# FNet mixing and an RWKV channel mix in one kernel: K by whole pieces, two small operations moved between engines, one pair of gathers gated, some value products earlier

## The chip, the cores and the metric

The kernel runs on one NeuronCore of a Trainium2 chip. The metric is the device time of one execution, in microseconds. The core has five engines with a queue of instructions each: TensorE (PE in the profile, with its weight loads as PEld), VectorE (DVE), ScalarE (ACT), GpSimd (POOL) and SyncE (SP, here for output transfers only). Each works through its own queue in order and waits on semaphores for the others. Data moves between memory and the chip by 16 DMA engines; the transfers issued by GpSimd go through one queue (q0), those by SyncE through another (q1). TensorE writes into PSUM; VectorE and ScalarE carry results from there to SBUF ("evict").

## The reference, cut to what matters

```python
def _attn_ref(x):                       # x: (8, 3072, 256)
    X = np.fft.fft(x, axis=1)
    X = np.fft.fft(X, axis=2)
    return X.real.astype(np.float32)

def _moe_ref(x, mu_k, mu_r, w_k, w_v, w_r):
    x_prev = np.concatenate([np.zeros((B, 1, D)), x[:, :-1, :]], axis=1)
    xk = mu_k * x + (1.0 - mu_k) * x_prev
    xr = mu_r * x + (1.0 - mu_r) * x_prev
    k = np.maximum(xk @ w_k, 0.0)       # w_k: (256, 1024)
    v = k * k @ w_v                     # w_v: (1024, 256)
    r = 1.0 / (1.0 + np.exp(-(xr @ w_r)))   # w_r: (256, 256)
    return (r * v).astype(np.float32)
```

The output of the first function is the x of the second. The real part of a two-dimensional Fourier transform is taken for each of 8 batches, neighbouring rows are mixed, and a squared-ReLU layer with a sigmoid gate follows.

## The kernel before

**The transform.** It is done with matrix products and symmetry. The sequence of 3072 is split as 48 x 64. For each batch the rows of x and their mirror images are added (`fold`, into the tile p, VectorE), multiplied by tables of cosines and sines over the 48 (`a_sum`, `a_item`, `a_half`: into the tile a), multiplied by tables over the 256 columns (`d_units`, `d_item`, `d_small`: into g_all), and multiplied by tables over the 64 (`c_sums`, `c_item`, `c_pairs`: into y, which has 27 slots of 2 x 64 columns). `turned` repairs one column of g_all by a permutation. `evac` copies PSUM to SBUF on VectorE ("V") or ScalarE ("A"). Neighbouring slots of y are subtracted (`diff`, into d), scaled by mu (`scaled`, into t) and combined (`mixed`, into the tiles x), which gives xk and xr in transposed form, 128 partitions by 2 halves by 1536 columns; the "halves" are the two halves of the 256 columns of the model.

**The tables** are made on the chip at the start: angles are formed from small matrix products in PSUM, scaled and offset to a whole number of turns, wrapped by a bit-and, and put through the sine. `m_angles` (VectorE) does the first 6 of 14 angle blocks, `m_angles_2` the other 8, whose PSUM tile has 512 columns; each has two operations, one for the cosine and one for the sine (c = 0, 1). `wrap_angles` is the bit-and on both, `m_sine` the sine. All small VectorE operations of this kind are recorded with line 277 (`ts`), copies with 520 and 522 (`evac`).

**The layer.** Each batch has 6 chunks of 512 rows. A chunk takes four steps; in each step `k_piece` makes one quarter of K (two column blocks of w_k, each with the two halves of xk: 4 matmuls of 512 columns, line 758), ScalarE applies the ReLU from PSUM (line 779), and VectorE, or ScalarE in a few steps, squares it (lines 789, 787). The value products w_v of a chunk follow about 5 steps later: `v_tile` (line 810, 8 matmuls of 256 columns) for one block of 128 rows, or, for the first chunks, `v_part` (line 822), which takes one quarter of K for all blocks as soon as it is squared: 8 matmuls, or 4 where only two blocks are done so. `r_item` (lines 796, 801) makes the receptance gate of a chunk. `v_out` multiplies both and sends the result out.

**The first chunk** is special. Its first 256 columns need only the first slots of y, so `k_early` makes K products for columns 0 to 256 before the loop, and for 256 to 512 at steps 0 and 1. The order goes by halves: the first half of x for the pieces 0 and 1, then the second half for both. The x of the first 128 + 128 columns is written by four operations on line 905 (for each half two), and that of the columns 256 to 512 by line 723, one operation for each half.

**The order of work.** The program is one long straight list; `pin_order` keeps each engine's order as written. Before the loop everything is written out by hand. In the loop, `at(step, f)` puts an item into a step and `event(step, ...)` a group of TensorE items behind its value products; an event with over two items (unless it begins with `a_slots_0`) also adds the next step to the set `early_v`, which makes that step's `v_tile` come at the end of the step before. The order of a step is: K, items of kind x, value products (`v_tile`, then `v_part`), events, the value products brought forward, items of kind w, outputs, squares. The value products of steps 15 to 18 are `v_part` of the fourth chunk, that of step 19 its `v_tile` for block 2.

**Buffers.** PSUM has three tiles of 1024 columns (psW, `ps_w`), taken in turn by K, the receptance and the transform items, and two of 512 (psV, `ps_v`), taken in turn by value products and small items. A tile is taken again when its last reader is done.

**Weights.** `loads` (line 452), called between the first transform operations, puts on POOL's queue: two gathers of w_k (`wk`, by rows, line 140), a small memset, the transfer of w_v (line 456), two gathers of w_r (`wr`, line 140) and `half_rows`, a table (lines 493, 494) that step 3 needs. `load_gate` (line 464) is a way to time POOL's transfers: VectorE sets one element, and a POOL iota that overwrites it must wait for that; what is queued behind it on POOL starts no sooner. `loads_1` and `loads_2` are called at steps 1 and 4.

Of the kernel before, what the change touches and what calls it, by code (L numbers as in the profile page):

```python
# [13 lines left out]
AF = mybir.ActivationFunctionType  # L14
# [6 lines left out]
def _v(ap, extra_offset, free_dims):  # L21
    new_ap = [list(ap.ap[0])] + [[s, c] for (s, c) in free_dims]
    return dataclasses.replace(ap, offset=ap.offset + extra_offset, ap=new_ap)
# [16 lines left out]
def kernel(  # L40
# [10 lines left out]
    nc = tc.nc  # L51

    B, S, D = x.shape
# [52 lines left out]
    V = nc.vector  # L106
# [32 lines left out]
    def gather(dst, src, idx):  # L139
        nc.gpsimd.indirect_dma_start(dst, None, src, bass.IndirectOffsetOnAxis(ap=idx, axis=0))  # L140
# [47 lines left out]
    wr_sb = [[const.tile([P, 256], FP16, name=f"wr{m}{a}") for a in range(2)] for m in range(2)]  # L188
# [10 lines left out]
    TURN = 1 << 22  # L199
# [50 lines left out]
    row_i = const.tile([P, 4], UINT32)  # L250
# [24 lines left out]
    def ts(out, in0, s1, op0, s2=None, op1=None):  # L275
        kw = {} if op1 is None else {"op1": op1}
        V.tensor_scalar(out=out, in0=in0, scalar1=s1, scalar2=s2, op0=op0, **kw)

    MUL, ADD = ALU.mult, ALU.add
# [47 lines left out]
    for i in range(2):  # L327
        nc.scalar.activation(out=unit[:, i:i + 1], in_=g_i[0:2], func=AF.Copy, bias=1.0 - i,
                             scale=2.0 * i - 1.0)
# [31 lines left out]
    ph_c = const.tile([P, 4], FP32)  # L361
# [41 lines left out]
        ts(ang[:, :, j0:j1], ang[:, :, j0:j1], TURN - 1, ALU.bitwise_and)  # L403

    def m_angles_2(ps, j0, j1):
        for c in range(2):
            nc.scalar.activation(out=ang[:, c, j0:j1], in_=ps[:, 0:64 * (j1 - j0)],
                                 func=AF.Identity, bias=ph_c[:, 2 * c:2 * c + 1],
                                 scale=float(TURN) / S)

    def m_angles(ps, j0, j1, z=0):
        for c in range(2):
# [39 lines left out]
    def loads():  # L452
        for a in range(2):
            gather(wk_sb[0][a], moe_w_k, row_i[:, a:a + 1])
        m_first()
        nc.gpsimd.dma_start(out=wv_sb, in_=moe_w_v.rearrange("(fc p) v -> p fc v", p=128))
        for a in range(2):
            gather(wr_sb[0][a], moe_w_r, row_i[:, a:a + 1])
        half_rows()


# [2 lines left out]
    def load_gate():  # L464
        V.memset(gate, 0)  # L465
        iota(gate, pattern=[[0, 1]], base=0, channel_multiplier=0)  # L466

    def loads_1():
        load_gate()
# [48 lines left out]
    def evac(out_ap, in_ap, eng):  # L518
        if eng == "V":
            V.tensor_copy(out=out_ap, in_=in_ap)  # L520
        else:
            nc.scalar.activation(out=out_ap, in_=in_ap, func=AF.Copy)  # L522
# [86 lines left out]
    def d_evac(ps, u0, n, bank, eng):  # L609
        evac(_v(g_all, 256 * u0, [(64, 2), (128, 2 * n), (1, 64)]),  # L610
             _v(ps, 0, [(bank, 2), (64, 2 * n), (1, 64)]), eng)
# [135 lines left out]

    k2_t, st = {}, {}

    def k_products(c, ds, lo=0, hi=512, halves=(0, 1)):  # L750
        b, m, i = c
        xk = x_t[b, 0, m]
        if lo == 0 and halves[0] == 0:
            st["k", ds] = ps_w()
        for hs in range(2):
            fc = 2 * ds + hs
            for a in halves:
                nc.tensor.matmul(out=st["k", ds][:, 512 * hs + lo:512 * hs + hi],  # L758
                                 lhsT=wk_sb[m][a][:, 128 * fc:128 * fc + 128],
                                 rhs=xk[:, a, 512 * i + lo:512 * i + hi],  # L760
                                 start=(a == 0), stop=(a == 1))


    def k_early(lo, hi, which):
        for a, ds in which:
            k_products(chunks[0], ds, lo, hi, (a,))

    def k_piece(c, ds):
        if ds == 0:
            k2_t[c] = k2_pool.tile([P, 8, 512], FP16, name="k2", tag="k2")  # L770
            st["rl"] = k2_pool.tile([P, 8, 512], FP16, name="rl", tag="rl")
        if c == chunks[0] and ds < 2:
            if ds == 0:
                k_early(256, 512, ((0, 0), (0, 1), (1, 0)))
            else:
                k_early(256, 512, ((1, 1),))
        else:
            k_products(c, ds)
        nc.scalar.activation(out=st["rl"][:, 2 * ds:2 * ds + 2],  # L779
                             in_=st["k", ds].rearrange("p (f t) -> p f t", f=2),  # L780
                             func=AF.Relu, bias=0.0, scale=0.25)
# [21 lines left out]
    def v_tile(c, tb):  # L803

        apart = c == chunks[-1] and tb >= 2
        h = 0 if apart else tb % 2
        if h == 0:
            st["v", tb] = ps_v()
        for fc in range(8):
            nc.tensor.matmul(out=st["v", tb - h][:, 256 * h:256 * h + 256],  # L810
                             lhsT=k2_t[c][:, fc, 128 * tb:128 * tb + 128],
                             rhs=wv_sb[:, fc], start=(fc == 0), stop=(fc == 7))
# [3 lines left out]
    def v_part(c, ds, tbs):  # L816
        for tb in tbs:
            h = tb % 2
            if ds == 0 and h == 0:
                st["v", tb] = ps_v()  # L820
            for fc in (2 * ds, 2 * ds + 1):
                nc.tensor.matmul(out=st["v", tb - h][:, 256 * h:256 * h + 256],  # L822
                                 lhsT=k2_t[c][:, fc, 128 * tb:128 * tb + 128], rhs=wv_sb[:, fc],
                                 start=fc == 0 and h == 0, stop=fc == 7, skip_group_check=True)
# [60 lines left out]
    w, first = ps_w(), ps_w()  # L885
# [8 lines left out]
    turned(2, 4, small[1][:, 256:258], "V")  # L894
    d_evac(fill[:, 256:1024], 4, 1, 512, "A")
    d_evac(fill[:, 384:1024], 5, 1, 512, "V")
    x_t[0, 0, 0] = mix_pool.tile([P, 2, 1536], FP16, name="x00")
    for a in range(2):
        t = x_t["t", a] = mix_pool.tile([P, 24, 64], FP16, name=f"t{a}")
# [17 lines left out]
    keep_busy(NF[6], w[:, 768:1024], 256)  # L917
    c_sums((even, odd), 9, 8, 1)
    y_evac(0, 5, 4, w)
    evac(y[:, 4].rearrange("p a t -> p (a t)"), first[:, 256:384], "A")  # L920
    for z, p in enumerate((odd, even)):
        evac(_v(y, 128 * (9 + z), [(256, 4), (1, 128)]), p, "VA"[z])

# [5 lines left out]

    early_v = set()

    def event(step, *items):
        work.setdefault((step, "e"), []).extend((f[0], f[1:]) for f in items)
# [20 lines left out]
    for n, c in enumerate(chunks[:EARLY]):  # L958
        o_steps[4 * n + SHORT + 3] = [(c, 1, 2), (c, 3, 2)]
    o_steps[4 * EARLY + SHORT + 3] = [(chunks[EARLY], 1, 2)]  # L960
    k_early(0, 256, ((0, 0), (0, 1), (1, 0), (1, 1)))
    diff(0, 4, 8)
    mix_part(0, 0, 4, 8)
    y_evac(0, 0, 4, first)
# [77 lines left out]
    for b in range(B):  # L1042
# [8 lines left out]
        t = b + 2  # L1051
# [29 lines left out]
    for step in range(nk + LAG):  # L1081
        if step < nk:
            k_piece(chunks[step // 4], step % 4)
        due(step, "x")
        v = v_steps.get(step)
        if v and step not in early_v:
            v_tile(*v)
        if step in p_steps:
            v_part(*p_steps[step])
        due(step, "e")  # L1090
        if step + 1 in early_v:
            v_tile(*v_steps[step + 1])
        early = step in OUT_FIRST
        for v in o_steps.get(step, ()) if early else ():
            v_out(*v)
        due(step, "w")
        for v in () if early else o_steps.get(step, ()):
            v_out(*v)
        if step < 4 * EARLY + 4:
            square(chunks[step // 4], step % 4, 1, step in SQUARE_A)  # L1100
        elif step < nk and step % 2:
            square(chunks[step // 4], step % 4)
# [32 lines left out]
```

## Time and profile before

| | us |
|---|---|
| median of three runs | 432.34 |
| the three runs | 432.31, 432.34, 433.6 |
| the profiled execution: its time | 431.6 |
| the profiled execution: its span (first to last instruction) | 429.8 |

| engine | busy us | share of the span |
|---|---|---|
| TensorE | 422.8 | 98% |
| VectorE | 359.8 | 84% |
| ScalarE | 321.6 | 75% |
| GpSimd | 63.9 | 15% |

In the quoted rows a line gives the start and the length in microseconds, the engine, the line of the kernel, the operation, what it writes and reads, the size and how many like operations were merged (x8), and in brackets how long the engine was idle just before and what released it. "PEld" rows are weight loads, which run beside the matmuls. A transfer's row on POOL is the time in which POOL writes its descriptors; the data lands later. A matmul's length includes its way through the array, so matmuls that follow each other without a pause overlap in the rows.

### The profile page before, as it was taken

The page shows a single profiled execution, that of the slowest core. Times are in us where ns is not written, and L with a number is a line of the kernel's source. Part 1 is how long each engine was busy: PE and PEld are TensorE (multiplying, and loading weights), DVE is VectorE, ACT ScalarE, POOL GpSimd, SP SyncE. Part 2 cuts the span into 40 slices and gives each one's busy share as a digit, 9 for nine tenths or more (in the row PEclk, how much of TensorE's full clock was granted, in tenths as well). Part 3 has the DMA queues.
Part 4 walks back from the last instruction along what each step waited for, and adds up shares of the span by engine and source line. Part 5 has one row for each costly group of instructions (what it writes and reads, how often), then busy time and mean ns, then how long its engine had stood idle before and what let it go on. Part 6 is the DMA issues. An engine that isn't in the chain of part 4 may idle for free.

```text
span 429.8 us, 9299 instructions
## 1 busy us (share of the span) xinstructions
PE 422.8 (98%) x3858; PEld 298.5 (69%) x3858; DVE 359.8 (84%) x545; ACT 321.6 (75%) x376; POOL 63.9 (15%) x94
## 2 busy tenths in 40 slices
PE   8999999999999999999999999999999999999996
PEld 3667776777777776776677777777767767766765
DVE  8889989997998889988898988989799847997453
ACT  8889897877878678776777777777786867666661
POOL 7568402000050002300041000500000000000000
PEclk9999999999999999999999999999999999999999
DMA  8879946322385233933258223773232322223233
GB/s 173 113 117 195 229 116 130 75 56 68 70 153 143 52 77 65 197 83 72 57 116 187 57 54 73 133 159 75 52 72 50 76 65 60 69 64 72 67 73 99
DMA packets 35102, 42.06 MB, mean 98 GB/s; under 512 B 4114, under 2 KB 31092, under 8 KB 35060
## 3 DMA queue, kind: packets, MB, share of 16 engines
q1 hardware_dynamic: 27488, 25.41, 23.9%
q0 software_dynamic: 7264, 15.80, 22.0%
q8 instruction: 30, 0.49, 0.5%
q10 hardware_dynamic: 308, 0.26, 0.2%
q14 instruction: 12, 0.10, 0.1%
HBM read 32.08 MB, written 25.17 MB: 133 GB/s over the span
## 4 chain that ended last, share of the span: by engine, by line
PE 93%; POOL 2%; DMA 2%; issue 0%; DVE 0%; ACT 0%
PE psW L758 38%; PE psV L810 36%; PE psW L796 10%; PE psV L822 3%; PE psW L605 2%; DMA wv_sb<-in_moe_w_v_dram 2%; PE psW L679 1%; PE psW L565 1%; POOL xm L140 1%; PE psW L647 1%; POOL wk L140 1%; PE psW L583 0%; ACT rl L779 0%; POOL row_i L242 0%; PE psW L542 0%
## 5 line engine op out<-in xcount | busy, mean ns | idle before, releaser
L779 ACT ACTIVATE rl<-psW 128x1024 f16<-128x1024 f32 x192 | 195.2, 1025 | 92.2 <-PE psW L758 88.6
L758 PE MATMUL psW<-x,wk 128*128 128x512 f16 (+1 forms) x776 | 195.3, 377 | 0.6 <-DVE x L723 0.4
L810 PE MATMUL psV<-wv_sb,k 128*128 128x256 f16 x1424 | 184.1, 273 | 0.0
L810 PEld LDWEIGHTS <-k 128*128 128x128 f16 x1424 | 137.0, 98 | 35.7
L789 DVE TENSOR_TENSOR k<-rl 128x2048 f16<-128x2048 f16 (+1 forms) x100 | 115.6, 1157 | 33.7 <-ACT rl L779 33.3
L758 PEld LDWEIGHTS <-wk 128*128 128x128 f16 x776 | 74.8, 98 | 53.2 <-issue 1.1
L832 DVE SCALAR_TENSOR_TENSOR o<-psV,r 128x512 f32<-128x512 f32 (+1 forms) x97 | 65.8, 681 | 14.8 <-PE psV L810 13.4
L723 DVE TENSOR_TENSOR x<-y,t 128x1536 f16<-128x1536 f16 (+3 forms) x74 | 62.1, 845 | 2.1
L796 PE MATMUL psW<-wr,x 128*128 128x256 f16 x384 | 49.8, 273 | 0.0
L801 ACT ACTIVATE r<-psW 128x1024 f16<-128x1024 f32 x48 | 48.9, 1018 | 0.8 <-PE psW L796 0.8
L796 PEld LDWEIGHTS <-x 128*128 128x128 f16 x384 | 37.5, 98 | 14.3 <-issue 0.2
L466 POOL IOTA gate<- 1x1 int32 x6 | 2.1, 356 | 202.4 <-DVE gate L465 202.4
L522 ACT ACTIVATE a<-psW 128x832 f16<-128x832 f32 x31 | 25.9, 863 | 1.4 <-PE psW L565 1.4
L522 ACT ACTIVATE g_all<-psW 128x1024 f16<-128x1024 f32 (+5 forms) x37 | 25.6, 693 | 0.4 <-PE psW L628 0.2
L140 POOL DMA_INDIRECT xm<-in_x_dram,idx_g x18 | 22.9, 1271 | 5.5 <-issue 5.2
L171 DVE TENSOR_TENSOR p<-xp,xm 112x2304 f16<-112x2304 f16 (+6 forms) x19 | 21.6, 1138 | 0.0
L712 DVE TENSOR_SCALAR t<-d,muf_t 128x1536 f16<-128x1536 f16 (+3 forms) x42 | 21.2, 518 | 0.1
L712 DVE TENSOR_SCALAR t<-d,mu_m 128x1536 f16<-128x1536 f16 x32 | 19.7, 616 | 0.0
L605 PEld LDWEIGHTS <-a 128*128 128x128 f16 x208 | 14.0, 98 | 6.8 <-ACT a L522 0.7
L182 DVE TENSOR_TENSOR eo<-p 112x1152 f16<-112x1152 f16 (+3 forms) x28 | 17.9, 679 | 0.0
L700 DVE TENSOR_TENSOR d<-y 128x1664 f16<-128x1664 f16 (+5 forms) x19 | 16.7, 881 | 0.7 <-ACT y L522 0.7
L522 ACT ACTIVATE pq<-psW 128x1024 f16<-128x1024 f32 (+1 forms) x18 | 15.2, 880 | 2.3 <-PE psW L679 2.3
(137 smaller groups left out, 219.6 us busy)
## 6 DMA issues: line engine op xcount, KB each, us to landing
out_dram<-o SPq DMA_DIRECT2D x189, 128.0 KB, 2.4
xp<-in_x_dram POOLq DMA_DIRECT2D x12, 216.0 KB, 4.5
xp<-in_x_dram POOLq DMA_DIRECT2D x13, 192.0 KB, 6.9
xp<-in_x_dram POOLq DMA_DIRECT2D x2, 384.0 KB, 6.6
wv_sb<-in_moe_w_v_dram POOLq DMA_DIRECT2D x1, 512.0 KB, 9.6
xp<-in_x_dram SPq DMA_DIRECT2D x1, 480.0 KB, 4.0
xp<-in_x_dram POOLq DMA_DIRECT2D x1, 432.0 KB, 4.8
xm<-in_x_dram,idx_g POOLq DMA_INDIRECT x18, 7.8
```

What stands on the lines that cost most here:

```text
L140: nc.gpsimd.indirect_dma_start(dst, None, src, bass.IndirectOffsetOnAxis(ap=idx, axis=0))
L522: nc.scalar.activation(out=out_ap, in_=in_ap, func=AF.Copy)
L605: nc.tensor.matmul(out=ps[:, o:o + 128], lhsT=a_t[b][:, e, 2 * (u0 + i):2 * (u0 + i) + 2, :], rhs=w_eo[:, e], start=True, stop=True)
L712: V.tensor_scalar(out=dst, in0=src, scalar1=mu, scalar2=None, op0=ALU.mult)
L723: V.tensor_tensor(out=_v(x_t[b, j, m], o, [(64 * step, hi - lo), (step, 64)]), in0=y_t[b][:, lo + 3 * m:hi + 3 * m, a], in1=x_t["t", a][:, ...
L758: nc.tensor.matmul(out=st["k", ds][:, 512 * hs + lo:512 * hs + hi], lhsT=wk_sb[m][a][:, 128 * fc:128 * fc + 128], rhs=xk[:, a, 512 * i + l ...
L779: nc.scalar.activation(out=st["rl"][:, 2 * ds:2 * ds + 2], in_=st["k", ds].rearrange("p (f t) -> p f t", f=2), func=AF.Relu, bias=0.0, sca ...
L789: V.tensor_tensor(out=k2_t[c][:, lo:hi], in0=r, in1=r, op=ALU.mult)
L796: nc.tensor.matmul(out=ps[:, 256 * tb:256 * tb + 256], lhsT=x_t[b, 1, m][:, a, 512 * i + 128 * tb: 512 * i + 128 * tb + 128], rhs=wr_sb[m] ...
L801: nc.scalar.activation(out=st["r", c], in_=ps, func=AF.Sigmoid)
L810: nc.tensor.matmul(out=st["v", tb - h][:, 256 * h:256 * h + 256], lhsT=k2_t[c][:, fc, 128 * tb:128 * tb + 128], rhs=wv_sb[:, fc], start=(f ...
L832: V.scalar_tensor_tensor(out=o.rearrange("p a b -> p (a b)")[:, 0:256 * n], in0=st["v", t0][:, 0:256 * n], scalar=16.0, in1=st["r", c][:, ...
```

## The change

There are five edits.

- `m_angles_2`: the operation for c = 1 goes from ScalarE to VectorE.
- Of the evictions of the first batch's y, slot 4 (128 columns) goes from ScalarE to VectorE, and the odd ones of slots 9 to 15 (512 columns) from VectorE to ScalarE, ahead of the even ones, which are there already.
- The K products of the first chunk run piece by piece: for each column block both halves of x in turn, all of piece 0 and then all of piece 1, for columns 0 to 256 and again for 256 to 512. `k_early` and the argument `halves` go.
- The two gathers of w_r leave `loads` for a new function `loads_0`, which begins with `load_gate` and is called behind the evictions of the units 4 and 5. `half_rows` stays in `loads` and so comes ahead of them.
- `early_v` begins with the steps 17, 18 and 19, and the rule for it now takes `v_part` too.

```diff
     def m_angles_2(ps, j0, j1):
-        for c in range(2):
-            nc.scalar.activation(out=ang[:, c, j0:j1], in_=ps[:, 0:64 * (j1 - j0)],
-                                 func=AF.Identity, bias=ph_c[:, 2 * c:2 * c + 1],
-                                 scale=float(TURN) / S)
+        nc.scalar.activation(out=ang[:, 0, j0:j1], in_=ps[:, 0:64 * (j1 - j0)],
+                             func=AF.Identity, bias=ph_c[:, 0:1], scale=float(TURN) / S)
+        ts(ang[:, 1, j0:j1], ps[:, 0:64 * (j1 - j0)], float(TURN) / S, MUL, ph_c[:, 2:3], ADD)
...
         nc.gpsimd.dma_start(out=wv_sb, in_=moe_w_v.rearrange("(fc p) v -> p fc v", p=128))
-        for a in range(2):
-            gather(wr_sb[0][a], moe_w_r, row_i[:, a:a + 1])
         half_rows()
...
+    def loads_0():
+        load_gate()
+        for a in range(2):
+            gather(wr_sb[0][a], moe_w_r, row_i[:, a:a + 1])
...
-    def k_products(c, ds, lo=0, hi=512, halves=(0, 1)):
+    def k_products(c, ds, lo=0, hi=512):
...
-            for a in halves:
+            for a in range(2):
...
-        if c == chunks[0] and ds < 2:
-            if ds == 0:
-                k_early(256, 512, ((0, 0), (0, 1), (1, 0)))
-            else:
-                k_early(256, 512, ((1, 1),))
-        else:
-            k_products(c, ds)
+        k_products(c, ds, 256 if c == chunks[0] and ds < 2 else 0)
...
     d_evac(fill[:, 384:1024], 5, 1, 512, "V")
+    loads_0()
...
-    evac(y[:, 4].rearrange("p a t -> p (a t)"), first[:, 256:384], "A")
+    evac(y[:, 4].rearrange("p a t -> p (a t)"), first[:, 256:384], "V")
     for z, p in enumerate((odd, even)):
-        evac(_v(y, 128 * (9 + z), [(256, 4), (1, 128)]), p, "VA"[z])
+        evac(_v(y, 128 * (9 + z), [(256, 4), (1, 128)]), p, "A")
...
-    early_v = set()
+    early_v = set(range(17, 20))
...
-    k_early(0, 256, ((0, 0), (0, 1), (1, 0), (1, 1)))
+    k_products(chunks[0], 0, 0, 256)
+    k_products(chunks[0], 1, 0, 256)
...
-        if step in p_steps:
+        if step in p_steps and step not in early_v:
             v_part(*p_steps[step])
         due(step, "e")
         if step + 1 in early_v:
-            v_tile(*v_steps[step + 1])
+            if step + 1 in v_steps:
+                v_tile(*v_steps[step + 1])
+            if step + 1 in p_steps:
+                v_part(*p_steps[step + 1])
```

More of the change, by code (lines that the diff above doesn't have):

```diff
@@ L748 @@
     k2_t, st = {}, {}
-    def k_products(c, ds, lo=0, hi=512, halves=(0, 1)):
+    def k_products(c, ds, lo=0, hi=512):
         b, m, i = c
         xk = x_t[b, 0, m]
-        if lo == 0 and halves[0] == 0:
+        if lo == 0:
             st["k", ds] = ps_w()
@@ L761, in k_products @@
                                  start=(a == 0), stop=(a == 1))
-    def k_early(lo, hi, which):
-        for a, ds in which:
-            k_products(chunks[0], ds, lo, hi, (a,))
     def k_piece(c, ds):
```

## Prediction

> **What bounds the kernel now.** I read the page's first lines and its chain first, then stages of the span, then the waits of TensorE, and last the order of time where TensorE stood still.
>
> ```profile
> span 429.8 us, 9299 instructions
> PE 93%; POOL 2%; DMA 2%; issue 0%; DVE 0%; ACT 0%
> ```
>
> TensorE sets the end. A stage row gives its length, then the busy time of PE, PEld, DVE, ACT and POOL, the clock, the DMA share and GB/s:
>
> ```profile
> 18.00:23.38 5.38, 4.61 (x39) 2.94 (x35) 5.31 (x17) 4.79 (x10) 0.57 (x2) 1.00 0.77 98
> 23.38:50.00 26.62, 26.62 (x225) 19.15 (x225) 24.87 (x53) 23.44 (x27) 20.78 (x27) 1.00 0.99 184
> 50.00:60.00 10.00, 9.88 (x108) 6.97 (x107) 9.04 (x14) 9.03 (x13) 0.00 (x0) 1.00 0.80 185
> 60.00:425.00 365.00, 365.00 (x3360) 260.04 (x3359) 304.99 (x390) 269.23 (x291) 28.39 (x36) 1.00 0.40 87
> ```
>
> The clock is full, and between 23.38 and 425 us TensorE's record has one hole, 0.12 us between 50 and 60 (a matmul's end is modelled and drawn over the next start, so the real hole is somewhat larger). No edit removes a matmul, so time can come from two places only: that hole, and the moment at which the unbroken run begins. What releases that moment stands in the chain in order of time (start, length, what):
>
> ```profile
> 13.76 9.57 DMA wv_sb<-in_moe_w_v_dram
> ...
> 25.46 0.87 PE psV L822 x8
> ```
>
> and in the order of time around it:
>
> ```profile
> 21.08 1.97 PE L758 MATMUL psW<-x,wk 128*128 128x512 f16 x8
> ...
> 22.42 1.30 DVE L789 TENSOR_TENSOR k<-rl 128x1024 f16<-128x1024 f16 x2
> ...
> 23.16 0.97 PEld L822 LDWEIGHTS <-k 128*128 128x128 f16 x8 [0.61 <-DVE gate L465]
> ...
> 23.38 1.03 PE L822 MATMUL psV<-wv_sb,k 128*128 128x256 f16 x8 [0.33 <-DMA wv_sb<-in_moe_w_v_dram]
> ```
>
> The first value products (L822, step 3) need three things: TensorE free of the K products (drawn until 21.08 + 1.97 = 23.05), the first square of VectorE (its weights load at 23.16), and w_v, issued at 13.76, landed at 13.76 + 9.57 = 23.33. The transfer comes last, by 0.22 us over the square. Whatever is made faster ahead of it is worth at most 0.22 us unless the transfer lands earlier too. That is the point of the whole forecast.
>
> **The change part by part.**
>
> *Angle operation.* ScalarE loses one of two operations, VectorE gains one.
>
> ```profile
> 6.45 1.23 ACT L407 ACTIVATE rl<-psV,ph_c 128x512 int32<-128x512 f32 x2
> ...
> 6.65 0.59 DVE L277 TENSOR_SCALAR rl<-rl 128x768 int32<-128x768 int32 x1
> ...
> 7.72 0.69 DVE L277 TENSOR_SCALAR rl<-rl 128x1024 int32<-128x1024 int32 x1 [0.48 <-ACT rl L407]
> ...
> 11.70 2.35 ACT L522 ACTIVATE a<-psW 128x832 f16<-128x832 f32 x3
> ...
> 14.54 0.40 PE L605 MATMUL psV<-w_eo,a 128*128 128x128 f16 x4 [0.23 <-ACT a L522]
> ...
> 18.32 0.68 DVE L520 CAST y<-psV 128x512 f16<-128x512 f32 x1
> ```
>
> ScalarE gains 1.23 / 2 = 0.61 us. VectorE's new operation reads 512 columns of PSUM; the nearest row is the 0.68 us cast of L520. VectorE is free at 6.65 + 0.59 = 7.24, and 0.48 us of waiting goes, so its chain slips by between 0 (operations overlapping) and 0.2 us. ScalarE's lead runs on to the evictions at 11.70, which start as it comes free; the last piece of a waits for TensorE and VectorE too, so I take about half of the 0.61, 0.3 us, at the matmuls of 14.54 (bounds 0 and 0.6).
>
> *Slots.* VectorE loses the 512-column cast and gains a 128-column copy; ScalarE the reverse.
>
> ```profile
> 16.53 0.42 DVE L520 CAST g_all<-psW 128x256 f16<-128x256 f32 x1
> ...
> 17.27 1.13 DVE L905 SCALAR_TENSOR_TENSOR x<-psW,muf_t,t 128x128 f16<-128x128 f32 x4 [0.33 <-ACT t L900]
> ...
> 18.43 0.28 ACT L522 ACTIVATE y<-psW 128x128 f16<-128x128 f32 x1 [0.31 <-DVE x L905]
> 18.61 0.59 ACT L522 ACTIVATE y<-psV 128x512 f16<-128x512 f32 x1
> ...
> 19.05 0.61 PE L605 MATMUL psV<-w_eo,a 128*128 128x128 f16 x8
> ...
> 19.77 0.48 DVE L723 TENSOR_TENSOR x<-y,t 128x256 f16<-128x256 f16 x2
> ...
> 20.10 1.03 PE L758 MATMUL psW<-x,wk 128*128 128x256 f16 x8 [0.44 <-DVE x L723]
> ```
>
> From 0.42 (256 columns) and 0.68 (512) follow 0.26 us per 256 columns, so 0.29 for 128: VectorE gains 0.68 - 0.29 = 0.39 us. ScalarE pays 0.59 - 0.28 = 0.31, mostly out of the 0.31 us that it waited. The K products of 20.10 waited 0.44 us for VectorE, so this gain reaches them and the squares behind them: the first square would release at 23.16 - 0.39 - (0 to 0.3) = 22.5 to 22.8.
>
> *K one whole piece at a time.* Same matmuls, other order: the second one already needs the second half of x. In the first group the halves come from L905, four operations over 1.13 us, so the second matmul waits for about the last half of that, some 0.4 us less the 0.2 us that two matmuls took in between: the group ends up to 0.3 us later. In the second group the second half of x comes 0.48 / 2 = 0.24 us after the first. Against that, the first piece is complete after four matmuls instead of six, 2 x 0.11 = 0.22 us sooner, for the ReLU. The 0.44 us of waiting ahead of 20.10 hides the first loss; without that cover it costs the 0.3. I take zero.
>
> *Gated gathers.* The two gathers of w_r leave POOL's queue behind w_v; the order table (POOL, under 1 us) moves ahead of them, and they wait for a VectorE memset placed behind the cast of 16.53, hence at 16.53 + 0.42 = 16.95.
>
> ```profile
> 13.76 1.21 POOL L456 DMA_DIRECT2D wv_sb<-in_moe_w_v_dram  x1
> ...
> 15.27 0.98 POOL L140 DMA_INDIRECT wr<-in_moe_w_r_dram,row_i  x1 [0.30 <-issue]
> ...
> 16.56 0.94 POOL L140 DMA_INDIRECT wr<-in_moe_w_r_dram,row_i  x1 [0.30 <-issue]
> ...
> 27.69 1.04 PE L796 MATMUL psW<-wr,x 128*128 128x256 f16 x8
> ...
> 34.22 1.93 POOL L140 DMA_INDIRECT wr<-in_moe_w_r_dram,row_i  x1 [0.30 <-issue]
> ```
> ```profile
> L466 POOL IOTA gate<- 1x1 int32 x6 | 2.1, 356 | 202.4 <-DVE gate L465 202.4
> ```
> ```profile
> DMA to landing us min/median/max: 7.4/8.3/8.7
> ```
> ```profile
> 16.50:18.00 1.50, 1.44 (x28) 0.98 (x27) 1.17 (x6) 1.28 (x4) 1.29 (x3) 1.00 0.96 114
> 18.00:20.00 2.00, 1.66 (x20) 1.28 (x17) 1.97 (x8) 1.69 (x5) 0.45 (x1) 1.00 1.24 154
> ...
> 21.00:22.00 1.00, 1.00 (x8) 0.47 (x6) 1.00 (x4) 1.00 (x2) 0.00 (x0) 1.00 0.34 46
> 22.00:23.40 1.40, 1.07 (x6) 0.40 (x5) 1.40 (x5) 1.40 (x3) 0.12 (x1) 1.00 0.19 25
> ```
>
> The gate adds 0.36 us on POOL, so the gathers start near 17.4 and 18.7, 2.1 us later than now. Behind them on POOL stands only the next gate, which waits for VectorE until 23.05 anyway. The receptance products need w_r at 27.69; landing rows of w_r (7.4 to 8.7 us, the line of its tile) bound it at 27.4, so there is just room. Does w_v land earlier? The stages show a tail: 154 GB/s until 20, then 46 and 25. A few of the 16 DMA engines finish late, and w_r, 15.27 + 8.3 = 23.6, landed just behind w_v, not among it. Nothing ahead of w_v in the queue is changed, so the lower end is no gain. The upper end is the landing no longer deciding: then the square does, at 22.5, a gain of 23.38 - 22.55 = 0.83 us. The other end is a loss: if the transfer stands still while POOL writes the two gathers, now in its midst, it lands 0.98 + 0.94 = 1.92 us later. I take a gain of 0.25 us, near the lower end, because less is queued while the tail runs.
>
> A rule of the Trainium skill speaks against this edit: DMA: Bandwidth & Descriptors, section Queues, rings and completion order, says that each DMA engine takes descriptors in ring order, and its section SWDGE vs HWDGE vs iDMA that the GpSimd path has one context. By it what stands behind w_v cannot hold it up, and this term would be 0 instead of 0.25, the sum 0.28 and the time 432.1. The landing of w_r behind w_v agrees with it.
>
> *Value products of steps 17 to 19 ahead.*
>
> ```profile
> 52.66 1.02 ACT L779 ACTIVATE rl<-psW 128x1024 f16<-128x1024 f32 x1 [0.26 <-PE psW L758]
> ...
> 53.01 0.60 PE L822 MATMUL psV<-wv_sb,k 128*128 128x256 f16 x4
> ...
> 53.73 1.02 PE L758 MATMUL psW<-x,wk 128*128 128x512 f16 x4
> ...
> 55.85 1.23 DVE L789 TENSOR_TENSOR k<-rl 128x2048 f16<-128x2048 f16 x1 [0.60 <-ACT rl L779]
> ```
>
> A value matmul streams 0.87 / 8 = 0.109 us (chain row of 25.46), so four from 53.01 end at 53.45; K of step 17 starts at 53.73, when the ReLU has emptied its PSUM buffer (52.66 + 1.02 = 53.68). The hole is 0.28 us. With the four value matmuls of step 17 moved there (0.44 us), K starts at 53.89: the hole is gone, and K, its ReLU and the square come 0.16 us later. That square already waited 0.60 us, and it is read by value products of later steps. The inputs of the moved products are squares of steps 12 to 15, long done. Gain 0.28; bounds +0.28 and, if the later K makes a new hole, -0.16.
>
> *Sum.* 0.25 + 0.28 = 0.53 us against the span of 429.80. That execution took 431.6 us, and the median of the three runs, 432.34, stands 0.74 above it; applied to the median: 432.34 - 0.53 = **431.8 us**. A difference of under 0.3%, 1.30 us here, is about what a measurement of this kernel cannot tell from none.
>
> **The rivals.**
>
> *R1, w_v no longer decides:* the transfer lands before 22.5, since the gathers are out of its way. For it: the rate falls to 114 GB/s in the stage in which the second gather is written. Against: that stage is also the end of w_k, and the tail. Time: 432.34 - 0.83 - 0.28 = 431.2. Another 0.2 us, from a K order or a ScalarE lead that is worth its upper bound, takes it past the 0.3%.
>
> *R2, slower:* the gathers are written in the midst of w_v's transfer and stop it, 1.92 us. Time: 432.34 + 1.92 - 0.28 = 434.0. It decides as soon as the landing slips by over 0.28, and is past 0.3% from 1.58 us on. For it: one w_r gather took 1.93 us (at 34.22) where the first two took 0.98 and 0.94, so the pair could even last longer. Against: 154 GB/s in 18 to 20, when a POOL operation ran as well.
>
> On R2 the Trainium skill, SBUF — State Buffer, section Who interferes with whom, says that VectorE in a two-port mode shuts GpSimd out of the port by which it writes descriptors. The gate moves the gathers beside more such VectorE work. The single row of 1.93 us would fit; no run here separates it.
>
> *R3, nothing is gained:* w_v lands as before, and the later K of step 17 gives the 0.28 back further on. For it: ScalarE and VectorE are 90% busy in 50 to 60. Against: the 0.60 us that the square waited. Time: 432.3 (to 432.5).
>
> **How the numbers follow.** Forecast 0.53, its own range 431.2 to 432.3; R1 0.19; R2 0.13; R3 0.15. Faster by over 0.3% (below 431.04) is most of R1 with its extra, and the spread between runs: 0.18. Slower by over 0.3% is R2 almost whole: 0.12. The rest, 0.70, is within. The range takes in R1 with its extra and most of R2 short of a full stop: 430.7 to 433.5.
>
> **What would show it.** Right: the first L822 matmuls still wait for w_v, by more than 0.33 us; K of step 17 follows the value products without a hole; the K products of 20.10 start about 0.4 us sooner; nothing else moves. R1: the wait of L822 for the DMA is gone and it starts before 22.7. R2: w_v's length in the chain is above 11 us, or the receptance products wait for w_r. R3: a new PEld or PE wait between 54 and 70. Wrong altogether would be a hole in the unbroken run after 60 us.

## The result and the profile after

| | before, us | after, us |
|---|---|---|
| median of eight runs each | 432.37 (432.26 to 433.63) | 431.30 (431.14 to 431.80) |
| the profiled execution: time, span | 431.6, 429.8 | 431.37, 429.6 |

The ratio after to before is 0.9968, 95% interval 0.9955 to 0.9980: faster by 0.9 to 1.9 us, by 1.07 us in the medians. The ratio moved further than the medians because three of the eight runs before took 433.6 us and none of those after took over 431.8. The two profiled executions differ by only 0.23 us. So most of the gain isn't between the two traces; where it comes from needed the experiments.

The stages of the profile after, in the columns explained with the prediction:

```profile
18.00:23.38 5.38, 5.12 (x43) 3.07 (x44) 5.19 (x18) 4.91 (x9) 1.56 (x2) 1.00 0.37 48
23.38:50.00 26.62, 26.62 (x226) 19.19 (x226) 25.09 (x53) 23.74 (x28) 20.80 (x28) 1.00 0.98 181
50.00:60.00 10.00, 10.00 (x111) 7.21 (x110) 8.89 (x14) 8.92 (x12) 0.00 (x0) 1.00 0.83 192
60.00:425.00 365.00, 365.00 (x3361) 259.98 (x3359) 305.46 (x391) 269.14 (x292) 28.39 (x36) 1.00 0.39 87
```

The hole between 50 and 60 is gone (10.00 busy of 10.00). In 18 to 23.38 the transfers are nearly done: 48 GB/s instead of 98. Its order of time, the lines that answer to those shown of before:

```profile
7.16 0.73 DVE L277 TENSOR_SCALAR rl<-psV,ph_c 128x512 int32<-128x512 f32 x1
...
7.44 0.65 POOL L242 IOTA row_i<- 64x2 uint32 x4
...
8.88 1.21 DVE L171 TENSOR_TENSOR p<-xp,xm 96x1024 f16<-96x1024 f32 x1
...
11.29 1.66 ACT L524 ACTIVATE a<-psW 128x832 f16<-128x832 f32 x2
...
12.27 0.95 POOL L455 DMA_DIRECT2D wv_sb<-in_moe_w_v_dram  x1
...
14.78 0.40 PE L607 MATMUL psV<-w_eo,a 128*128 128x128 f16 x4
...
17.57 1.04 POOL L140 DMA_INDIRECT wr<-in_moe_w_r_dram,row_i  x1 [0.17 <-issue]
...
18.27 1.33 PE L760 MATMUL psW<-x,wk 128*128 128x256 f16 x8
...
18.83 1.08 ACT L524 ACTIVATE y<-psV 128x512 f16<-128x512 f32 x2 [0.47 <-PE psV L649]
18.91 0.95 POOL L140 DMA_INDIRECT wr<-in_moe_w_r_dram,row_i  x1 [0.30 <-issue]
...
20.29 1.13 PE L760 MATMUL psW<-x,wk 128*128 128x256 f16 x8
...
23.36 1.05 PE L813 MATMUL psV<-wv_sb,k 128*128 128x256 f16 x8
...
53.11 1.04 PE L813 MATMUL psV<-wv_sb,k 128*128 128x256 f16 x8
53.98 1.03 PE L760 MATMUL psW<-x,wk 128*128 128x512 f16 x4
```

w_v is issued at 12.27 instead of 13.76, and no wait of the first value product (L813 here) for it is left; yet that product starts at 23.36, as before (23.38): the square now comes last. The same view from 14 to 24 us has its rows:

```profile
22.61 0.69 DVE L780 TENSOR_TENSOR k<-rl 128x1024 f16<-128x1024 f16 x1
...
23.35 0.66 PEld L813 LDWEIGHTS <-k 128*128 128x128 f16 x7 [0.41 <-DVE gate L462]
```

The first square ends at 23.30, and the weights made from it load at 23.35 (the gate named there is a memset of VectorE right behind the square). K of step 17 follows at 53.98, right behind the eight value products (53.11 + 8 x 0.109 = 53.98).

### The profile page after: what moved, and what is told of

It is laid out like the page before. It is cut to its first block, busy times and chain, and to the rows that moved or that the text cites. A ratio compares the mean times of both kernels' runs of the same rounds, so it can differ in the third digit from the quotient of the medians.

```text
span 429.6 us, 9302 instructions
## 1 busy us (share of the span) xinstructions
PE 423.4 (99%) x3858; PEld 298.4 (69%) x3858; DVE 360.4 (84%) x547; ACT 321.5 (75%) x375; POOL 62.4 (15%) x95
## 4 chain that ended last, share of the span: by engine, by line
PE 98%; DVE 1%; ACT 0%; issue 0%; POOL 0%
PE psW L760 39%; PE psV L801 37%; PE psW L787 10%; PE psV L813 3%; PE psW L607 3%; PE psW L681 1%; PE psW L567 1%; PE psW L206 1%; PE psW L585 1%; PE psW L649 1%; PE psV L347 1%; PE psV L649 0%; ACT y L524 0%; PE psV L585 0%; PE psV L607 0%
## 5 line engine op out<-in xcount | busy, mean ns | idle before, releaser
L770 ACT ACTIVATE rl<-psW 128x1024 f16<-128x1024 f32 x192 | 194.9, 1024 | 91.2 <-PE psW L760 87.3
L607 PEld LDWEIGHTS <-a 128*128 128x128 f16 x208 | 14.0, 98 | 6.7 <-ACT a L524 0.5
L182 DVE TENSOR_TENSOR eo<-p 112x1152 f16<-112x1152 f16 (+3 forms) x28 | 17.9, 679 | 0.0
```

Of the source, the lines that this page charges most:

```text
L607: nc.tensor.matmul(out=ps[:, o:o + 128], lhsT=a_t[b][:, e, 2 * (u0 + i):2 * (u0 + i) + 2, :], rhs=w_eo[:, e], start=True, stop=True)
L770: nc.scalar.activation(out=st["rl"][:, 2 * ds:2 * ds + 2], in_=st["k", ds].rearrange("p (f t) -> p f t", f=2), func=AF.Relu, bias=0.0, sca ...
```

## The experiments

There were three groups of four, each on one chip with its own runs of the kernel before: chip A (median before 432.43 us), chip B (432.98) and chip C (431.46). Ratios are against the kernel before on the same chip. This table is the key to all of them. It has each profiled execution's time, the start of its first value product, and the difference:

| kernel (chip) | time | first value product | difference |
|---|---|---|---|
| before, first profile | 431.60 | 23.38 | 408.22 |
| before, second profile (A) | 432.23 | 23.95 | 408.28 |
| gate alone (A) | 431.75 | 23.50 | 408.25 |
| angle alone (A) | 431.83 | 23.57 | 408.26 |
| products ahead alone (A) | 433.40 | 25.27 | 408.13 |
| K order alone (B) | 433.43 | 25.18 | 408.25 |
| slots alone (B) | 432.22 | 23.96 | 408.26 |
| two more gathers (B) | 436.09 | 27.83 | 408.26 |
| after | 431.37 | 23.36 | 408.01 |
| after, gate later (B) | 430.84 | 22.94 | 407.90 |
| after without the gate (C) | 431.58 | 23.63 | 407.95 |
| gate later, alone (C) | 431.39 | 23.15 | 408.24 |
| after, plain transfers added (C) | 431.15 | 23.19 | 407.96 |
| after, gate later, a difference moved (C) | 431.09 | 22.76 | 408.33 |

Whatever comes first, the rest takes 408.2 to 408.3 us without the products ahead, and 407.9 to 408.1 with them, but for the last row, which is taken up below. All other differences lie in the start. (The time is about 1.8 us more than the span in every profile, so that much of the difference lies outside the span.)

**The kernel before again** (chip A, unchanged, against itself).

> The kernel before, unchanged, against itself, to see how far its profiled execution stands for its timed ones. The profiled one took 431.6 us, all eight timed ones 432.26 or more. Theory W (the landing of w_v differs from execution to execution and sets the start of the unbroken run): a second profile shows the first L822 at another time than 23.38, and the execution's time moves with it, us for us. Rival N (the 0.7 us lie outside the start, in the output or the launch): the first L822 stays at 23.4 and the span outside it moves. Ratio 1.000.

Ratio 0.9999 (0.9989 to 1.0008). The second profile starts its value products 0.57 us later than the first, and its time is 0.63 us longer: theory W holds in that the start carries the time, but it is not w_v. TensorE's waits name no transfer any more; this stands in the order of time:

```profile
16.05 0.18 PE L628 MATMUL psV<-g_all,turn 128*128 128x2 f16 x1
...
16.40 0.95 POOL L140 DMA_INDIRECT wr<-in_moe_w_r_dram,row_i  x1 [0.30 <-issue]
17.15 0.17 DVE L520 CAST g_all<-psV 128x2 f16<-128x2 f32 x1 [0.84 <-PE psV L628]
17.18 0.84 ACT L900 ACTIVATE t<-psW,mu_n 128x256 f16<-128x256 f32 x2 [1.07 <-PE psV L628]
...
17.38 0.29 PE L647 MATMUL psW<-m_cs,g_all 64*128 64x128 f16 x4 [0.72 <-issue]
```

The matmul of L628 ends at 16.23, but VectorE and ScalarE, idle for 0.84 and 1.07 us and waiting for that alone, start at 17.15 and 17.18. TensorE itself stands idle for 0.72 us; this row names no releaser, but in the run with two more gathers the same wait (0.65 us, at 17.90) is put down to VectorE's cast. In the first profile of before the same three lines read:

```profile
16.23 0.18 PE L628 MATMUL psV<-g_all,turn 128*128 128x2 f16 x1
...
16.40 0.47 ACT L900 ACTIVATE t<-psW,mu_n 128x256 f16<-128x256 f32 x1
16.45 0.17 DVE L520 CAST g_all<-psV 128x2 f16<-128x2 f32 x1
```

There the followers start as the matmul ends (16.41). I call what the second one shows a late signal. It costs about 0.8 us where no engine has anything else to do: the first K products come at 18.81 instead of 18.04.

**The gate alone** (chip A): `loads_0` with `load_gate` and the two gathers, behind `d_evac(fill[:, 384:1024], ...)`, into the kernel before.

```diff
-        for a in range(2):
-            gather(wr_sb[0][a], moe_w_r, row_i[:, a:a + 1])
         half_rows()
...
+    loads_0()
```

> Before plus the gated w_r gathers alone. Theory G (the gathers, written while w_v is on its way, hold it up): no wait of L822 for w_v is left, the landing is before 22 and the time falls by 0.5 to 0.9 us (ratio 0.998 to 0.9988). Theory A (w_v is early in the changed kernel because POOL issued it at 12.27 instead of 13.76, and it did so because the angle operation on VectorE stopped blocking POOL): w_v is issued at about 13.8 as before, its tail stays, no change (ratio 1.000).

431.81 us, ratio 0.9985 (0.9976 to 0.9994). w_v was issued at 13.78, so theory A is not needed for this gain. Nor is theory G shown as it was put down there: in the second profile of before no value product waited for w_v either, so an earlier w_v does not explain the gain. From here on theory G stands for something else, that the gathers make the signals late.

```profile
16.23 0.18 PE L631 MATMUL psV<-g_all,turn 128*128 128x2 f16 x1
...
16.39 0.84 ACT L904 ACTIVATE t<-psW,mu_n 128x256 f16<-128x256 f32 x2
16.44 0.17 DVE L523 CAST g_all<-psV 128x2 f16<-128x2 f32 x1
...
18.64 0.69 DVE L523 CAST y<-psV 128x512 f16<-128x512 f32 x1 [0.25 <-PE psV L650]
```

The late signal at 16 us is gone; a smaller one stands at 18.64, where VectorE's cast of slots waited 0.25 us, just after the first gather, now written from 17.32 to 18.36.

**The angle operation alone** (chip A): the `m_angles_2` of the change.

```diff
-        for c in range(2):
-            nc.scalar.activation(out=ang[:, c, j0:j1], ...)
+        nc.scalar.activation(out=ang[:, 0, j0:j1], ...)
+        ts(ang[:, 1, j0:j1], ps[:, 0:64 * (j1 - j0)], float(TURN) / S, MUL, ph_c[:, 2:3], ADD)
```

> Before plus the angle operation on VectorE alone. Theory A: w_v is issued near 12.3 instead of 13.76, lands 1 to 1.5 us sooner, and the first L822 waits for the square instead, near 23.4: the time falls by 0.5 to 0.9 us (ratio 0.998 to 0.9988). Theory G: the issue may move but the gathers behind it still hold w_v up, and VectorE's folds start 0.2 us later as in the changed kernel: no gain or 0.2 us slower (ratio 1.000 to 1.0005).

432.35 us, ratio 0.9992 (0.9983 to 1.0001): no gain that can be told. Theory A is half right: POOL did issue w_v earlier, at 12.67, but a late signal stood at 15.98: the matmul ended at 15.64, and VectorE's cast, idle for 0.47 us, started 0.34 us behind it, beside the gathers, which had moved up too (the second was written from 15.22 to 16.16). An early w_v alone bought nothing that can be told here.

**The products of steps 17 to 19 ahead, alone** (chip A).

```diff
-    early_v = set()
+    early_v = set(range(17, 20))
```
(with the two conditions for `v_part` in the loop)

> Before plus the value products of steps 17 to 19 ahead, alone. Both theories: the hole ahead of K of step 17 (0.28 us) is gone, nothing else moves, ratio 0.9993 to 0.9995. If the later K gives it back, 1.000.

432.19 us, ratio 0.9995 (0.9986 to 1.0003), and 408.13 in the table: in line with the hole, though the interval holds 1. Its profiled execution is among its long ones (433.4) and shows a second cost, the granted clock (column after POOL):

```profile
20.00:21.00 1.00, 1.00 (x7) 0.69 (x6) 0.96 (x3) 1.00 (x3) 0.00 (x0) 0.50 1.09 143
21.00:22.00 1.00, 1.00 (x11) 0.94 (x10) 1.00 (x5) 0.35 (x2) 0.00 (x0) 0.50 0.19 25
22.00:23.00 1.00, 1.00 (x7) 0.76 (x6) 0.96 (x4) 0.90 (x2) 0.00 (x0) 0.51 0.00 0
23.00:24.00 1.00, 1.00 (x10) 0.70 (x9) 0.98 (x3) 0.67 (x1) 0.00 (x0) 1.00 0.00 0
```

One late signal, seen in two waits (VectorE 0.66, ScalarE 1.10 us near 17.9), left TensorE idle, its clock fell to 0.50 and came back at 23: the first value product starts at 25.27. The signal alone doesn't do it: the second profile of before had waits of 0.84 and 1.07 us, and its clock stayed at 1.00. In this execution TensorE was late before any gather of w_r was written: its eight matmuls of zeros at 6.08 took 3.50 us in all, against 2.34 in the first profile of before, and the products of L605 began at 15.03 instead of 14.54. The profile of the K order alone is of the same kind (3.33 us, then 0.50 from 20 to 22). In the timed runs of the kernel before on chips A and B, 17 of 58 took 433.0 us or more, all at a mean clock of 0.996; none of the 17 with the gate alone or the gate later did. The Trainium skill, TensorE: Matmul & The Clock Gate, section What's actually happening, has half the clock after an idle window of about 3.4 us and the full one after a busy window. The halving and the return agree; a whole idle window is not what came before: in 16 to 20 us TensorE's records fill 0.73, 0.40, 0.92 and 1.00 of each microsecond. Why those eight matmuls took longer in some executions is not shown.

**The K order alone and the slots alone** (chip B): `k_products` in place of `k_early`; and the engines of two evictions.

```diff
-    k_early(0, 256, ((0, 0), (0, 1), (1, 0), (1, 1)))
+    k_products(chunks[0], 0, 0, 256)
+    k_products(chunks[0], 1, 0, 256)
```
```diff
-    evac(y[:, 4]..., first[:, 256:384], "A")
+    evac(y[:, 4]..., first[:, 256:384], "V")
-        evac(_v(y, 128 * (9 + z), ...), p, "VA"[z])
+        evac(_v(y, 128 * (9 + z), ...), p, "A")
```

> Before plus K one whole piece at a time, alone. In the profiles so far the time is the start of the first value product plus 408.2 us whatever came before it, so only that start counts. Prediction's step (worth nothing, hidden by the wait for x): ratio 1.000. Rival: in executions in which w_v has landed in time, the two lost waits for the second half of x (0.3 us) push the first piece and the square: 0.1 to 0.3 us slower, ratio 1.0002 to 1.0007. A gain would mean that the earlier ReLU leads: 0.2 us, ratio 0.9995.

> Before plus the exchange of slot 4 and slots 9 to 15, alone. If VectorE's chain from the slots to the first square sets the start in the timed executions (as in the second profile of the kernel before, where the square came 0.06 us ahead of the first L822), its 0.39 us come out in full: ratio 0.9991. If w_v sets the start, as in the first profile, 0 to 0.1 us: ratio 1.000.

432.98 us, ratio 0.9996 (0.9985 to 1.0007), and 432.95, ratio 1.0002 (0.9989 to 1.0014): neither can be told from nothing here, and each interval holds both of the outcomes named beforehand. Both profiles have a late signal behind L628 (0.71 and 0.86 us in VectorE's wait). With the slots exchanged the second group of K products came 1.87 us after the first (19.02 and 20.89), against 2.07 in the second profile of before (18.81 and 20.88): 0.20 us.

**Two more gathers** (chip B): a double dose at the old place; their data is not used.

```diff
+        for a in range(2):
+            gather(spare[a], moe_w_r, row_i[:, a:a + 1])
         half_rows()
```

> Before with two more gathers of w_r into spare tiles, behind the two of w_r and ahead of half_rows (their data is not used): a double dose of what the gate moves away. Theory G (gathers written at 15 to 18 us stall the small evictions of the first batch: TensorE's signals reach ScalarE and VectorE 0.3 to 0.9 us late while they run): the stalls go on to 20 us, start 0.4 to 1 us later, ratio 1.001 to 1.0023. Theory Q (a queue served in order: what stands behind w_v holds up nothing): ratio 1.000.

435.97 us, ratio 1.0057 (1.0039 to 1.0075): 3 us slower, more than theory G asked for. Theory Q falls.

```profile
17.36 0.94 POOL L140 DMA_INDIRECT spare<-in_moe_w_r_dram,row_i  x1 [0.30 <-issue]
...
18.46 0.17 PE L631 MATMUL psW<-g_all,turn 128*128 128x4 f16 x1
...
18.61 0.94 POOL L140 DMA_INDIRECT spare<-in_moe_w_r_dram,row_i  x1 [0.31 <-issue]
...
20.63 0.19 ACT L525 ACTIVATE g_all<-psW 128x4 f16<-128x4 f32 x1 [2.08 <-remote]
...
21.51 0.69 DVE L523 CAST y<-psV 128x512 f16<-128x512 f32 x1 [1.80 <-PE psV L650]
...
23.76 0.60 ACT L525 ACTIVATE g_all<-psV 128x512 f16<-128x512 f32 x1 [1.14 <-PE psV L608]
```

The eviction behind L631 starts 2.0 us after the matmul's end at 18.63, with the extra gathers written from 17.36 to 19.55. So it outlasts the writing by 1.1 us, and the order table that GpSimd makes next ends at 20.50: the writing of the gathers itself is not singled out. The waits at 21.51 and 23.76 follow from this one and from the clock, which was at 0.50 from 20 to 26 us and so has its part in the 3 us.

**The gate 2 us later** (chip B): the changed kernel with `loads_0()` behind the first `diff`.

```diff
     diff(0, 4, 8)
+    loads_0()
     mix_part(0, 0, 4, 8)
```

> The changed kernel with the gate and the w_r gathers 2 us later still, behind the first difference of slots (L702), near 19.5 us. Theory G: the late signal at 18.3 to 18.8 us (ScalarE's eviction of slots 9 to 15 waited 0.47 us in the changed kernel) is gone, or sits at 20 to 21 us where it meets the ReLU: start 0.2 to 0.4 us sooner or the same, time 430.9 to 431.4. Theory Q: no change, 431.3, as long as w_r lands before 27.8.

431.03 us, ratio 0.9955 (0.9942 to 0.9968).

```profile
16.22 0.18 PE L630 MATMUL psV<-g_all,turn 128*128 128x2 f16 x1
...
16.38 0.84 ACT L891 ACTIVATE t<-psW,mu_n 128x256 f16<-128x256 f32 x2
16.43 0.17 DVE L522 CAST g_all<-psV 128x2 f16<-128x2 f32 x1
...
18.12 1.08 ACT L524 ACTIVATE y<-psV 128x512 f16<-128x512 f32 x2
...
19.50 1.04 POOL L140 DMA_INDIRECT wr<-in_moe_w_r_dram,row_i  x1 [0.17 <-issue]
...
22.94 1.05 PE L813 MATMUL psV<-wv_sb,k 128*128 128x256 f16 x8
```

No signal is late in the stretch up to 19.5, not even the one of 0.47 us that the changed kernel has at 18.83, and the value products start 0.42 us sooner than there; 0.25 of that stands already at the products of L607 (14.53 instead of 14.78), ahead of all w_r gathers. The load on the DMA engines does not explain a late signal: from 16 to 18 us they moved 131 and 162 GB/s here, without one, and 142 and 98 GB/s in the slots alone, on the same chip, with one. Nor does the loading of instructions: in the run with the products ahead no packet of an instruction queue moved from 16.9 to 18.1 us, around its late signal. On the same chip, none, one and two pairs of gathers among the small evictions go with 431.03, 432.98 and 435.97 us (the first has the other edits too).

**The change without the gate, and the late gate alone** (chip C).

```diff
         nc.gpsimd.dma_start(out=wv_sb, ...)
+        for a in range(2):
+            gather(wr_sb[0][a], moe_w_r, row_i[:, a:a + 1])
...
-    loads_0()
```

> The changed kernel with the two w_r gathers back in loads, ahead of half_rows, the other four edits kept. Theory G: the gathers are written at about 13.8 to 16.2 us, TensorE's late signals return, and the time is that of before less the 0.24 us of the hole: ratio to before 0.999 to 0.9998. Rival A (the angle operation, by freeing POOL, is what brings the start forward): most of the change's gain stays, ratio 0.9965 to 0.9975.

> Before plus the gated gathers alone, at the later place (behind the first difference of slots, near 19.5 us). Theory G: no late signals before 19 us, first L822 when w_v has landed or the square is done, 23.2 to 23.4; the 0.28 us hole at step 17 stays. Time 431.3 to 431.7, that is most of the gain of the late gate with all edits. If the other edits carry the gain together with the gate, 432 or more.

430.93 us, ratio 0.9985 (0.9976 to 0.9994), and 431.47, ratio 1.0000 (0.9991 to 1.0009). Both are against expectation: the edits other than the gate gained 0.53 us, the late gate nothing. Its 431.47 lies in the range that theory G gave in microseconds, but the kernel before took no longer here. On chip C there seems to be no late signal to remove. The one profile there with the gathers ungated has

```profile
16.08 0.94 POOL L140 DMA_INDIRECT wr<-in_moe_w_r_dram,row_i  x1 [0.30 <-issue]
...
16.13 0.18 PE L627 MATMUL psV<-g_all,turn 128*128 128x2 f16 x1
...
16.35 0.17 DVE L519 CAST g_all<-psV 128x2 f16<-128x2 f32 x1 [0.17 <-PE psV L627]
```

with the cast right behind the matmul, while a gather is written beside it. That execution was the longest of its eleven (431.58), as VectorE waited 0.52 us for a gather of x at 11.68, ahead of this stretch. The 431.46 us before on this chip is 1.0 us under chip A, about what a late signal costs; the kernel before itself has no profile here. So gathers alone don't seem to be enough; what differs between the chips no run shows. The line of w_v's tile in these two kernels, first ungated, then gated:

```profile
DMA to landing us min/median/max: 8.2/8.2/8.2
```
```profile
DMA to landing us min/median/max: 8.2/8.2/8.2
```

That is no proof that what stands behind w_v in the queue leaves it alone. With something behind it the landing took 9.6 us (the first profile of before), 8.2 and 9.5 (the plain transfers below); with nothing close behind it 8.2 and 6.6 (the last run). The spread within each kind is as large as the difference between them. What is shown is that no value product waited for w_v in any profile but the first of before.

**Plain transfers in the gathers' place** (chip C): the changed kernel with two POOL transfers of the same size behind w_v, not by index; their data is not used.

```diff
         nc.gpsimd.dma_start(out=wv_sb, ...)
+        for a in range(2):
+            nc.gpsimd.dma_start(out=spare[a], in_=moe_w_r[128 * a:128 * a + 128, :])
```

> The changed kernel with two plain POOL transfers of the same size (128 rows of w_r each, into spare tiles, data not used) in the place from which the gathers were taken, directly behind w_v. Theory G in the form that gathers by index do it: no late signals, time 431.2 to 431.6 as the changed kernel. In the form that any descriptors written by POOL at that moment do it, or the 256 KB behind w_v: late signals at 14 to 17 us as in the kernel before, 431.8 to 432.8.

431.26 us, ratio 0.9999 (0.9990 to 1.0008), no late signal. It decides nothing, since this chip shows none with gathers either. Whether it takes a gather by index stays open.

**The late gate and a difference moved** (chip C).

```diff
-    at(0, diff, 0, 0, 4)
+    at(1, diff, 0, 0, 4)
```

> The changed kernel with the later gate and with the last small difference of slots (0.42 us on VectorE, line 702) moved from step 0 to step 1, behind the first square. In the run with the later gate the square released the first value product at 22.9 and TensorE was free at about 22.7: start 0.2 us sooner, time 430.7 to 430.9. If w_v's landing lies there too, no change against the run with the later gate.

431.03 us, ratio 0.9982 (0.9966 to 0.9998). The time missed the 430.7 to 430.9 that was expected. The start came at 22.76, 0.18 us before the run of the change with the later gate, as expected; but the rest took 408.33 us, because a hole opened ahead of

```profile
52.71 0.27 PE L607 MATMUL psW<-w_eo,a 128*128 128x128 f16 x2 [0.20 <-DVE g_all L522]
```

The row gives 0.20 us; as the record draws a matmul's end over the next start, the real hole is larger. The gain at the start was lost there in that execution. Among the versions tried, the change with the later gate has the best ratio, 0.9955, but on the chip where the kernel before is slowest; the change as it is was not run on chip B.

## Why the prediction was right, and where it was not

The time lay in the range, and a small gain was forecast. The sum was 0.53 us, the medians moved by 1.07: one term was mis-sized, and for a reason that the prediction did not have. The hit owes something to a wide range (430.7 to 433.5): the 431.30 is near the 431.2 of R1, whose mechanism did not come, and not near the 431.8 of the sum. Two of the prediction's signs of being right failed (a wait for w_v that stays; K products 0.4 us sooner, which came at 20.29 for 20.10). And the measurement tells this change from none, as its interval ends at 0.9980, where the prediction thought that 0.3% could not be told.

- *The unbroken run.* That time "can come from two places only" was right, and the table shows it over a spread of 4.9 us in the start.
- *The hole at step 17,* 0.28: right. The rest of the run shortened from 408.2-408.3 to 407.9-408.0 in the kernels with all edits, but for the one with a difference moved. R3 did not come: the later K made no new hole.
- *What sets the start.* This is the step that failed. "The transfer comes last, by 0.22 us over the square" was true of the one profiled execution of before, which took 431.6 us where all eight timed ones took over 432.2. The second profile of it, at 432.23 us near the medians, starts 0.57 us later by a late signal, and w_v is in time. The term of 0.25 us for the gated gathers measured 0.62 on chip A (432.43 to 431.81), by removing a stall of the small evictions and not by an earlier w_v, and nothing on chip C. The prediction saw 431.6 beside 432.34 and carried the difference along as it was; the second profile puts 0.57 us of it ahead of the first value product, inside the span.
- *R1* has one of its signs (no wait for w_v) without the other, a start before 22.7: w_v is early because POOL issued it 1.49 us sooner, and the square decides at 23.3. R1 priced the square at 22.5, with gains of VectorE that did not reach it.
- *R2* failed: with the gathers written in the midst of its transfer, w_v was not waited for in any profile, and the pair took 1.04 and 0.95 us in its new place, against 0.98 and 0.94. For the rule on ring order that the prediction cites from the Trainium skill (DMA: Bandwidth & Descriptors, section Queues, rings and completion order), the landings (8.2 us with and without gathers behind, 6.6 to 9.6 in all) decide nothing. On two chips the gathers do harm, but to TensorE's signals.
- *The angle operation.* Predicted 0.3 us sooner at L607; it was 0.24 later in that execution (14.78 for 14.54) and at 14.53 to 14.60 in four other profiles with this operation: no gain. The new operation took 0.73 us, not 0.68, and the folds began at 8.88 instead of 8.66: the loss of up to 0.2 that the prediction named came out in full. ScalarE was 0.41 us early at its evictions (11.29) but had to wait for TensorE behind those folds. What goes with it on POOL was not foreseen: in five of the six profiles with VectorE's new operation, the four small index operations (iota) of L242 are done in 0.65 or 0.66 us instead of 1.20, and w_v goes out at 12.27 to 12.73, 1.0 to 1.5 us sooner; in the sixth, the change without the gate, they took 1.22 us and w_v went out at 13.50. So the operation alone doesn't settle it.
- *Slots.* VectorE's 0.39 us gave 0.20 ahead of the second K group and nothing measurable in the time.
- *K order.* Worth nothing that can be told, as taken. The first group stretched from 1.05 to 1.33 us, the 0.3 that was named, and the wait behind it hid that.
- *The gate's own times.* Gathers predicted at 17.4 and 18.7, measured 17.57 and 18.91; w_r was in time.

Added up, the single edits' medians give 0.62 + 0.08 + 0.24 (chip A) + 0.00 + 0.03 (chip B) = 0.97 us of the 1.07, each with an interval of some 0.4 us either way. The closeness is partly luck: the terms come from two chips, no edit was run alone on the chip of the result, and on chip C the gate gave nothing and the other four together 0.53.

## What to carry to other kernels

Before a change is costed from one profiled execution, compare its time with the timed runs: here it was 0.7 us shorter, and what set the start in it was not what sets it usually. Where a kernel is one unbroken run of TensorE, subtract the start of that run from the time; if the rest is constant, only the start and the holes are worth work. Transfers that GpSimd writes while small evictions pass between engines can be moved to a stretch where nobody waits for a signal: it gave 0.62 us on one chip here and nothing on another, so the place is worth trying on more than one.

## What the runs showed of the hardware that was not expected

- TensorE's signal to VectorE and ScalarE came 0.3 to 2 us after the matmul's recorded end, on two chips of three, in stretches in which GpSimd wrote gathers by index or had just done so; a second pair cost 3 us, part of it through the clock, and none among the small evictions left no such wait. Why, and why not on the third chip, stays open; whether the matmul or only its signal was held cannot be read from these records, nor whether the writing or the gathers' data does it.
- Such a stall can cost twice: TensorE's granted clock fell to 0.50 and stayed there for some 3 us (20 to 23 us), and in the run with two more gathers for some 6. It need not: with waits of the same size the clock stayed at 1.00 in the second profile of before and in the slots alone.
- With a VectorE operation that reads PSUM in the place of a ScalarE one, GpSimd's queue was 1.0 to 1.5 us ahead in five profiles of six (four iotas in 0.65 us instead of 1.20; w_v's issue from 13.76 to 12.27 to 12.73), and only 0.26 in the sixth.
